# Two PSUM banks for the last down product, and an earlier place for the conditioning's tanh and SiLU

## Chip, cores and metric

The kernel runs on one core of a Trainium2 chip. The metric is the device time of one execution in microseconds. Seven runs of the kernel before had a median of 254.84 us, from 253.79 to 256.03 us. The profile shows one execution in detail; it took 254.04 us, and its span, the time from the first to the last profiled event, is 252.3 us.

## What is computed

One transformer block on 2048 tokens of width 448, in bf16, conditioned on one vector `c`:

```
mod = silu(c) @ w_mod                      # six vectors of 448: sa, ca, ga, sb, cb, gb
h = layernorm(x) * (1 + ca) + sa
x = x + ga * attention(h)                  # 16 heads of 28, four segments of 512 tokens,
                                           # causal softmax in a segment, linear memory between segments
h = layernorm(x) * (1 + cb) + sb
x = x + gb * ((sigmoid(h @ w_gate) * (h @ w_up)) @ w_down)     # 448 -> 1792 -> 448
```

Two places of it matter here. At the very start `silu(c)` has to be there before the first conditioning vectors can be made, and these are folded into the projection weights. At the very end the product with `w_down` gives the last rows of the output.

## The kernel before

**How the work is laid out.** The 2048 tokens are four segments of four tiles with 128 tokens each. TensorE, VectorE (DVE), ScalarE (ACT), GpSimd (POOL) and the DMA queues of SP (SyncE) and ACT are each given their instructions in the order in which the Python code runs; the order is written out by hand, and each engine works its own list strictly from the front. The ACT list holds both ScalarE's computations and the loads that ACT issues, so an ACT load that waits also holds back the ACT computations written behind it, and the other way round. In the middle of the kernel a list of filler jobs with costs (`fill`, `tick`, `later`) decides where projections and the gated product go between the attention steps; the change touches neither that list nor its costs.

**The start.** L106 and L104 issue the loads of `c` (tile `c_col`, on ACT) and of the first four tiles of `x` (tile `x_sb`: tiles 0 and 1 on SP, 2 and 3 on ACT). L120 loads the parts 1 and 0 of `w_mod` (tiles `wm1`, `wm0`), each half by SP and half by ACT. L151 to L153 load `A_wq` and `A_wk` into a corner of `wd_sb`: row blocks 0 and 1 of each by SP, blocks 2 and 3 of `A_wq` by ACT, and those of `A_wk` by SP. L139 and L140 load `A_wv`. L196 is `th = tanh(c/2)` on ScalarE. It is written behind all of these loads, so it stands behind ACT's two `A_wq` loads, and the table load that the first ScalarE function needs stands just ahead of it.

Meanwhile TensorE runs 20 matmuls on a constant (`warm_up`, L647) that no result depends on. DVE computes the LayerNorm statistics of the four tiles (L269 and L270, one pair for a tile), POOL turns them into 1/sqrt(var+eps) for two tiles at a time (L273 and L274), and DVE then runs `silu_ops` (L200 and L201: two operations on a 112x4 tile, which give `silu`). TensorE makes the first conditioning columns from `silu` and `wm1` (L228), DVE normalizes tiles 0 and 1 (L277), evacuates those columns (L240), normalizes tiles 2 and 3, and evacuates the second columns (L238, tile `sa_bf`). TensorE transposes the normalized tiles (L688), DVE scales the projection weights by the columns (`pad_copy`, L657) and copies transposed tiles (L306), TensorE multiplies `sa_bf` with the weights (`bias_rows`, L664), and the first projections follow (L343).

**DMA semaphores.** The loads share eight completion semaphores, taken in turn as the loads are written in the program. A load that takes a semaphore again waits until the earlier load with that semaphore has landed, and so do the engine and queue behind it. Which earlier load that is follows from the order in which the whole program is laid out, and is seen in the list of the built program's instructions.

**PSUM.** `ps_m` is a pool of four PSUM tiles of one bank each, which `m_f32` hands out in turn. A tile is handed out again when its readers have finished.

**The end.** `down(s, t)` multiplies the gated product of one tile of tokens with `w_down`: 14 matmuls (L574) into one PSUM tile `dp`, one DVE addition of the residual (L576), and one store (L577, on ACT in the last two segments). For the very last tile `n` is 2: columns 0 to 223 and then columns 224 to 447, each with 14 matmuls, an addition and a store of its own, both in the same `dp`.

Of the kernel before, what the change touches and what calls it, by code (L numbers as in the profile page):

```python
# [9 lines left out]
F32 = mybir.dt.float32  # L10
AF = mybir.ActivationFunctionType
# [6 lines left out]
def kernel(  # L18
# [16 lines left out]
    nc = tc.nc  # L35
# [7 lines left out]
    KP, NK = 112, 4  # L43
# [5 lines left out]
    scale = float(Dh) ** -0.5  # L49
# [10 lines left out]
    const = ctx.enter_context(tc.tile_pool(name="const", bufs=1))  # L60
# [6 lines left out]
    def m_f32(name):  # L67
        return ps_m.tile([P, 512], F32, tag="m", name=name)
# [23 lines left out]
    def need(*tags):  # L92
        for tag in tags:
            late_ = [d for d in deferred if d[3] == tag]
            if late_:
                print("forced", tag, len(late_), max(d[0] for d in late_) - clock[0])
            run_deferred(lambda d: d[3] == tag)


    c_col = const.tile([KP, NK], BF16)  # L100
# [14 lines left out]
    def load_wm(engs, j):  # L115
        t = wm_bufs[j % 2]
        n = NK // len(engs)
        for i, eng in enumerate(engs):
            k = slice(i * n, (i + 1) * n)
            eng.dma_start(t[:, 0:NK * D].rearrange("p (k n) -> p k n", n=D)[:, k, :], wmod_k[:, k, j * D:(j + 1) * D])  # L120
        return t

    wm_bufs = [wts.tile([KP, NK * D + DP - D], BF16, name=f"wm{i}") for i in range(2)]
    wm = {j: load_wm((nc.sync, nc.scalar), j) for j in (1, 0)}
    wq_sb = wts.tile([P, NK, H, HP], BF16)
    wk_sb = wts.tile([P, NK, H, HP], BF16)
    wv_sb = wts.tile([P, NK, D], BF16)
# [64 lines left out]
    coef = const.tile([P, 2, H], F32)  # L192


    th = const.tile([KP, NK], F32)
    nc.scalar.activation(th[:], c_col[:], AF.Tanh, scale=0.5)  # L196
    silu = const.tile([KP, NK], BF16)

    def silu_ops():
        nc.vector.tensor_scalar(th[:], th[:], 0.5, 0.5, op0=ALU.mult, op1=ALU.add)  # L200
        nc.vector.tensor_tensor(silu[:], th[:], c_col[:], ALU.mult)  # L201
# [13 lines left out]
    def mod_cols(jobs, cp=None):  # L215
        evac = cp is None
        cp = cp_of[0] = m_f32("cp") if evac else cp
        for j, vi in jobs:
            for kc in range(NK):
                for k in range(NK):  # L220
                    c0 = k * D + kc * P
                    if vi >= 2 and kc == NK - 1:
                        for r in (0, LW):
                            nc.tensor.matmul(cp[r:r + LW, vi * NK + kc:vi * NK + kc + 1], lhsT=wm[j][:, c0:c0 + LW],
                                             rhs=silu[:, k:k + 1], start=(k == 0), stop=(k == NK - 1),
                                             tile_position=(0, r))
                        continue
                    nc.tensor.matmul(cp[:, vi * NK + kc:vi * NK + kc + 1], lhsT=wm[j][:, c0:c0 + P],  # L228
                                     rhs=silu[:, k:k + 1], start=(k == 0), stop=(k == NK - 1))
        if evac:  # L230
            mod_evac(jobs)
# [331 lines left out]

    def down(s, t):
        need("wd")
        dp = m_f32("dps")
        i = s * TPS + t
        ot = work.tile([P, D], BF16, tag="ot", bufs=2)
        eng = nc.scalar if s >= NSEG - 2 else nc.sync
        n = 2 if i == NSEG * TPS - 1 else 1  # L570
        for h in range(n):
            c = slice(h * D // n, (h + 1) * D // n)
            for fc in range(NFC):
                nc.tensor.matmul(dp[:, c], lhsT=fT_of[(s, fc)][:, t * P:(t + 1) * P], rhs=wd_sb[:, fc, c],  # L574
                                 start=(fc == 0), stop=(fc == NFC - 1))
            nc.vector.tensor_tensor(ot[:, c], dp[:, c], x_sb[:, i, c], ALU.add)  # L576
            eng.dma_start(out_dram[i * P:(i + 1) * P, c], ot[:, c])  # L577
# [27 lines left out]
    def down_jobs(s):  # L605
        return [(NFC * MV, lambda t=t: down(s, t)) for t in range(TPS)]
# [66 lines left out]
    for t in range(TPS):  # L673
        ln0.stats(t)
        if t % 2:
            ln0.rstd(t - 1, t + 1)
    silu_ops()
    mod_cols(((1, 1),), warm[:, 2, :])
    for t in range(2):
        ln0.norm(t)  # L680
# [193 lines left out]
```

The softmax here doesn't subtract the row's maximum and nothing guards it: scores larger than these inputs give would overflow.

## Time and profile before

| what | value |
|---|---|
| median of seven runs | 254.84 us |
| the profiled execution | 254.04 us, span 252.3 us |
| TensorE matmuls busy | 240.4 us, 95% of the span |
| DVE, ACT, POOL busy | 173.6, 139.1, 73.9 us |
| granted TensorE clock | full in all 40 slices |
| DMA engines busy | 90% or more of each slice from 6.3 to 44 us, under half in nearly all after 57 us |
| `dps` matmuls of L574 | 238 recorded, 43.9 us |

Busy time says which engine the kernel leans on; it does not say what a change at one place is worth. For that one reads the timeline at that place: the start of each instruction, its length, and in square brackets how long the engine was idle just before it and what ended that. A row "x14" is fourteen instructions of one line merged. "ACTq" and "SPq" are the issue of DMAs, with the time that issuing takes; when the data lands is told by another view as a number of microseconds after the issue. Matmuls overlap in the pipeline, so a merged row's length is not the sum of its parts.

### The profile page before, as it was taken

The numbers are of one execution on the slowest core, as the hardware profiler recorded it, in microseconds if no ns is written. First come the engines' busy times: TensorE is split into PE (matmuls) and PEld (weight loads), VectorE is DVE, ScalarE is ACT, GpSimd is POOL, SyncE is SP. The second block draws the span as 40 slices with busy tenths as digits, with TensorE's granted clock in tenths as the row PEclk, the third lists the DMA queues.
The fourth block names the chain that finished last, engine by engine and source line by source line (L and its number), as shares of the span: only waits on it lengthen the run. The fifth ranks groups of instructions, "written<-read, shape, count | busy, mean of one in ns | idle before, by whom it ended". The sixth has DMA issues, their size and how long they took to land.

```text
span 252.3 us, 5315 instructions
## 1 busy us (share of the span) xinstructions
PE 240.4 (95%) x2059; PEld 114.5 (45%) x2083; DVE 173.6 (69%) x419; ACT 139.1 (55%) x173; POOL 73.9 (29%) x140
## 2 busy tenths in 40 slices
PE   7899998999987999999999999999999999999994
PEld 3434544446533435545443355454444455333453
DVE  6878799784887786589866766895555585544422
ACT  0458879978896977667285838543642300233200
POOL 4359144232553223344513141471120032000000
PEclk9999999999999999999999999999999999999999
DMA  5999999494034330103342110123110105000011
GB/s 149 284 256 245 355 279 128 87 190 66 3 62 68 62 43 2 23 0 63 80 97 42 26 23 0 25 42 88 50 22 3 21 3 137 19 0 0 3 36 36
DMA packets 41168, 19.66 MB, mean 78 GB/s; under 512 B 30008, under 2 KB 40248, under 8 KB 41144
## 3 DMA queue, kind: packets, MB, share of 16 engines
q1 hardware_dynamic: 38408, 17.61, 32.7%
q10 hardware_dynamic: 2736, 1.72, 2.3%
q8 instruction: 16, 0.26, 0.4%
q14 instruction: 8, 0.07, 0.1%
HBM read 10.67 MB, written 1.84 MB: 50 GB/s over the span
## 4 chain that ended last, share of the span: by engine, by line
PE 52%; DVE 7%; POOL 1%; issue 1%; DMA 1%; ACT 1%; DVEq 0%; POOLq 0%
PE ups L559 13%; PE dps L574 13%; PE gps L542 12%; PE gps L547 5%; PE acc L451 3%; PE pwo L510 2%; PE lg L424 2%; DVE fT L562 1%; DVE st L269 1%; DMA hT<-xn 1%; DVE x_sb L520 1%; DVE ot L576 1%; DVE t L482 1%; PE dM L397 1%; PE ups L547 1%
## 5 line engine op out<-in xcount | busy, mean ns | idle before, releaser
L427 ACT ACTIVATE pT<-lg 128x2048 bf16<-128x2048 f32 (+1 forms) x48 | 76.8, 1599 | 25.9 <-PE lg L424 25.5
L562 DVE SCALAR_TENSOR_TENSOR fT<-tt,ups 128x512 bf16<-128x512 f32 x56 | 37.3, 688 | 39.3 <-PE ups L559 37.5
L437 POOL TENSOR_SCALAR_AFFINE_SELECT pT<-pT 128x512 bf16<-128x512 bf16 x64 | 40.6, 650 | 69.1 <-ACT pT L427 69.1
L550 ACT ACTIVATE tt<-gps 128x512 f32<-128x512 f32 x56 | 30.4, 594 | 55.1 <-PE gps L547 55.1
L574 PE MATMUL dps<-wd_sb,fT 128*128 128x448 bf16 (+1 forms) x238 | 43.9, 341 | 0.5 <-DVE ot L576 0.5
L542 PE MATMUL gps<-hT,wg_sb 128*128 128x512 bf16 x155 | 40.1, 379 | 1.4 <-ACT vt L357 0.6
L559 PE MATMUL ups<-hT,wu_sb 128*128 128x512 bf16 x165 | 40.6, 381 | 0.4 <-issue 0.3
L574 PEld LDWEIGHTS <-fT 128*128 128x128 bf16 x238 | 22.9, 98 | 19.4 <-issue 0.6
L559 PEld LDWEIGHTS <-wu_sb 128*128 128x128 bf16 x168 | 14.1, 97 | 21.7 <-issue 7.9
L542 PEld LDWEIGHTS <-wg_sb 128*128 128x128 bf16 x168 | 15.6, 98 | 18.2 <-DVE hT L291 1.1
L451 PE MATMUL acc<-vt,pT 128*128 128x29 bf16 x640 | 18.6, 175 | 2.1 <-POOL pT L437 1.7
L269 DVE BATCH_NORM_STATS2 st<-x_sb 128x6 f32<-128x448 bf16 x32 | 19.7, 617 | 0.5
L451 PEld LDWEIGHTS <-pT 128*128 128x128 bf16 x640 | 17.6, 96 | 5.2 <-POOL pT L437 2.4
L547 PE MATMUL ups<-hT,wgu_sb 64*128 64x512 bf16 x56 | 17.8, 382 | 0.8 <-ACT tt L550 0.5
L273 POOL TENSOR_SCALAR rs<-mv 128x1 f32<-128x1 f32 (+2 forms) x21 | 5.2, 247 | 44.6 <-DVE mv L270 44.1
L424 PE MATMUL lg<-qT,kT 28*128 28x512 bf16 (+3 forms) x256 | 17.3, 302 | 0.2
L547 PE MATMUL gps<-hT,wgu_sb 64*128 64x512 bf16 x56 | 17.0, 381 | 0.1
L343 PE MATMUL pq<-hT,wq_sb 128*128 128x512 bf16 x59 | 16.3, 379 | 0.7 <-issue 0.3
L576 DVE TENSOR_TENSOR ot<-dps,x_sb 128x448 bf16<-128x448 f32 (+1 forms) x17 | 9.9, 592 | 9.6 <-PE dps L574 9.6
L343 PE MATMUL pq<-hT,wk_sb 128*128 128x512 bf16 x62 | 16.3, 379 | 0.1
L277 DVE TENSOR_SCALAR xn<-x_sb,mv,rs 128x448 bf16<-128x448 bf16 x32 | 14.4, 472 | 2.1 <-POOL rs L274 2.0
L274 POOL TENSOR_TENSOR rs<-rs,mhalf 128x1 f32<-128x1 f32 (+2 forms) x21 | 14.3, 682 | 1.7
(101 smaller groups left out, 256.2 us busy)
## 6 DMA issues: line engine op xcount, KB each, us to landing
wm<-in_w_mod_dram SPq DMA_DIRECT2D x4, 392.0 KB, 6.5
x_sb<-in_A_x_dram SPq DMA_DIRECT2D x3, 448.0 KB, 7.3
wd_sb<-in_B_w_down_dram SPq DMA_DIRECT2D x3, 448.0 KB, 9.0
wg_sb<-in_B_w_gate_dram SPq DMA_DIRECT2D x3, 448.0 KB, 10.3
wu_sb<-in_B_w_up_dram SPq DMA_DIRECT2D x3, 448.0 KB, 10.9
out_dram<-ot SPq DMA_DIRECT2D x8, 112.0 KB, 1.9
out_dram<-ot ACTq DMA_DIRECT2D x7, 112.0 KB, 1.7
wm<-in_w_mod_dram SPq DMA_DIRECT2D x2, 196.0 KB
```

The costliest lines, as they stand in the source:

```text
L269: nc.vector.bn_stats(st[:], self.srcs[i])
L343: nc.tensor.matmul(pq[:, 0:L], lhsT=head_cols(w_sb, k, hc), rhs=h[:, k, :], start=(k == 0), stop=(k == NK - 1))
L424: nc.tensor.matmul(lg[:, hs, wid:wid + nq], lhsT=kT[r, hc, kb * P:(kb + 1) * P], rhs=qT[r, hc, kb * P:L], start=True, stop=True, tile_posi ...
L427: nc.scalar.activation(pT[:, :, w0:w0 + wid], lg[:, :, 0:wid], AF.Exp, scale=scale)
L437: nc.gpsimd.affine_select(out=blk, in_=blk, compare_op=ALU.is_ge, fill=0.0, base=0, pattern=[[0, 4], [1, P]], channel_multiplier=-1)
L451: nc.tensor.matmul(accv[:, qb, hs, 0:ME], lhsT=pT[:, hs, c0:c0 + P], rhs=vt[:, kb, hc * 4 + hs, 0:ME], start=(kb == 0), stop=(kb == qb))
L542: nc.tensor.matmul(g[:, 0:L], lhsT=wg_sb[:, k, f], rhs=h[:, k, :], start=(k == 0), stop=False)
L547: nc.tensor.matmul(dst[:, 0:L], lhsT=wgu_sb[r:r + LW, f], rhs=h[r:r + LW, 3, :], start=first, stop=not first, tile_position=(r, 0))
L550: nc.scalar.activation(tt[:], g[:, 0:L], AF.Tanh, scale=0.5)
L559: nc.tensor.matmul(u[:, 0:L], lhsT=wu_sb[:, k, f], rhs=h[:, k, :], start=False, stop=(k == 2))
L562: nc.vector.scalar_tensor_tensor(ft[:], tt[:], 1.0, u[:, 0:L], op0=ALU.add, op1=ALU.mult)
L574: nc.tensor.matmul(dp[:, c], lhsT=fT_of[(s, fc)][:, t * P:(t + 1) * P], rhs=wd_sb[:, fc, c], start=(fc == 0), stop=(fc == NFC - 1))
```

## The change

Three edits. The tanh of the conditioning vector moves from behind all loads to just behind the `w_mod` loads, so that in ACT's list it stands ahead of the two `A_wq` loads. `silu_ops` moves in DVE's list from behind the statistics of tile 3 to behind those of tile 1 (and the POOL operations of tiles 0 and 1). And in `down` the PSUM tile is taken inside the loop over the halves, so that the last tile's two halves have a PSUM bank each. No instruction is added or removed.

```diff
     wm = {j: load_wm((nc.sync, nc.scalar), j) for j in (1, 0)}
+    th = const.tile([KP, NK], F32)
+    nc.scalar.activation(th[:], c_col[:], AF.Tanh, scale=0.5)
     wq_sb = wts.tile([P, NK, H, HP], BF16)
...
-    th = const.tile([KP, NK], F32)
-    nc.scalar.activation(th[:], c_col[:], AF.Tanh, scale=0.5)
     silu = const.tile([KP, NK], BF16)
...
     def down(s, t):
         need("wd")
-        dp = m_f32("dps")
         i = s * TPS + t
...
         for h in range(n):
             c = slice(h * D // n, (h + 1) * D // n)
+            dp = m_f32("dps")
             for fc in range(NFC):
                 nc.tensor.matmul(dp[:, c], lhsT=fT_of[(s, fc)][:, t * P:(t + 1) * P], rhs=wd_sb[:, fc, c],
                                  start=(fc == 0), stop=(fc == NFC - 1))
...
         ln0.stats(t)
         if t % 2:
             ln0.rstd(t - 1, t + 1)
-    silu_ops()
+        if t == 1:
+            silu_ops()
     mod_cols(((1, 1),), warm[:, 2, :])
```

## Prediction

> **What bounds the kernel now.** The page first. TensorE is busy for 95% of the span and the granted clock is full throughout, so what TensorE waits for at the two places of the change is nearly all that can be won or lost.
>
> ```profile
> PE 240.4 (95%) x2059; PEld 114.5 (45%) x2083; DVE 173.6 (69%) x419; ACT 139.1 (55%) x173; POOL 73.9 (29%) x140
> PEclk9999999999999999999999999999999999999999
> L574 PE MATMUL dps<-wd_sb,fT 128*128 128x448 bf16 (+1 forms) x238 | 43.9, 341 | 0.5 <-DVE ot L576 0.5
> ```
>
> The last row says that all the down matmuls together have 0.5 us of idle time before them, and one releaser: the DVE addition of L576. The timeline of the end (start, length, then the idle time before and what ended it) shows where that is.
>
> ```profile
> 247.24 0.39 DVE L576 TENSOR_TENSOR ot<-dps,x_sb 128x224 bf16<-128x224 f32 x1 [0.72 <-PE dps L574]
> 247.68 1.50 PE L574 MATMUL dps<-wd_sb,fT 128*128 128x224 bf16 x14 [0.48 <-DVE ot L576]
> 249.22 0.39 DVE L576 TENSOR_TENSOR ot<-dps,x_sb 128x224 bf16<-128x224 f32 x1 [1.59 <-PE dps L574]
> ```
>
> TensorE finishes the first half, stands still while DVE adds it, and only then begins the second half. The chain of waits runs through exactly these three rows to the end.
>
> At the start I read the timeline of the first 16 us, engine by engine.
>
> ```profile
> 4.80 0.36 ACTq L152 DMA_DIRECT2D wd_sb<-in_A_wq_dram  x1
> 6.18 0.53 ACTq L153 DMA_DIRECT2D wd_sb<-in_A_wq_dram  x1
> 6.42 0.35 SPq L152 DMA_DIRECT2D wd_sb<-in_A_wk_dram  x1
> 6.74 1.28 ACT L196 ACT_TABLE_LOAD   x1 [6.74 <-DMA x_sb<-in_A_x_dram]
> 8.04 0.20 ACT L196 ACTIVATE th<-c_col 112x4 f32<-112x4 bf16 x1
> 8.05 0.18 DVE L270 BATCH_NORM_AGGREGATE mv<-st 128x2 f32<-128x6 f32 x1
> 8.27 0.17 DVE L200 TENSOR_SCALAR th<-th 112x4 f32<-112x4 f32 x1
> 8.56 0.70 DVE L277 TENSOR_SCALAR xn<-x_sb,mv,rs 128x448 bf16<-128x448 bf16 x2
> 8.64 0.88 POOL L274 TENSOR_TENSOR rs<-rs,mhalf 128x2 f32<-128x2 f32 x1
> 8.69 0.54 PE L228 MATMUL warm<-silu,wm 112*128 112x1 bf16 x16 [0.99 <-DVE silu L201]
> 9.56 0.70 DVE L277 TENSOR_SCALAR xn<-x_sb,mv,rs 128x448 bf16<-128x448 bf16 x2
> 10.72 0.16 DVE L238 CAST sa_bf<-warm 128x4 bf16<-128x4 f32 x1 [0.46 <-PE warm L228]
> 12.32 0.32 DVE L657 TENSOR_SCALAR wq_sb<-wd_sb,cols 64x448 bf16<-64x448 bf16 x1
> ```
>
> The tanh is late because ACT first has to issue two loads, which themselves wait. TensorE's 0.99 us of idle time looks like the prize, but DVE is the engine without slack here: it works almost without a gap from 5.26 us to 10.26 us, and what it gains counts. From L238 on, DVE runs nearly back to back to 14.3 us and TensorE follows it.
>
> **The end: one PSUM bank for each half.** Removed: the wait of 0.48 us. The second half's first matmul then follows the first half's last at the matmul pitch. Its PSUM tile is the one that `down` of the last segment's first tile used, and the addition that frees it ran at 240.6 us (an L576 row of the same timeline, 0.62 us long), 6 us earlier. So the 14 matmuls begin near 247.22 instead of 247.68: 0.46 us. The first half's addition (0.39 us) now lies beside the 1.50 us of matmuls; without that cover it would cost what it does now. The additions do not collide on DVE (the first ends at 247.63, the second would begin near 248.76), nor do the stores on ACT's queue: an L577 issue takes 0.34 us, the first at about 247.7 and the second at 249.1. What is late next is unchanged: the second addition, its store, 1.6 us to landing, the end. The bounds are 0.40 and 0.48; an addition of 0.62 us runs beside the matmuls of the next tile in the whole tiles just before, where L574 shows no gap. Taken: -0.46.
>
> **The start: ACT.** The tanh waits for `c_col`, which landed 4.0 us after its issue at 0.79. In the list of the built program the table load carries no wait, so it runs when the second `w_mod` issue is over (1.80 + 1.00 = 2.80) and ends at 4.1; the tanh then runs from 4.8 to 5.0, where it was done at 8.24. [...] The trace has 1.28 us and the tanh 0.02 us behind it. [...]
>
> **The two ACT loads behind the tanh.** More changes here than their place. The semaphores are taken in another order, so the loads wait for other landings. Block 2 of `A_wq` waited for `c_col` (issued 4.80); it now waits for SP's half of `wm1`, which released SP's L152 at 6.42: 1.6 us later. Block 3 waited for `x` tiles 2 and 3 (6.18); it now waits for SP's half of `wm0`, which landed between 6.4 and 8.2 (SP's L139, which waited for it, was issued at 8.21 straight behind the issue before it): 0.2 to 2.0 us later. In return the three `A_wk` loads wait for `c_col` and the two `x` loads and go to about 4.8, 5.2 and 6.2 from 4.98, 6.42 and 7.60, and `A_wv` to 7.6 from 8.21. They all lie ahead of their users by more than before. Block 2 is read at 11.74 and block 3 at 12.32 (L657), and by TensorE's L664 from 11.68 on. Before, these two took 4.9 and 4.6 us from issue to landing. With those rows block 2 lands at 11.3, in time, and block 3 at 11.0 to 12.8, up to 0.5 us late. [...] The last earlier one on ACT, its half of `wm0`, had landed by 8.8 (SP's L140, which waited for it, was issued at 8.83). [...] Taken: 0; the far end +0.5 stays for the range.
>
> **DVE, POOL and TensorE at the start.** In the statistics the next operation starts 0.10 us after an aggregate starts. Before, the first SiLU operation started 0.22 us after one (8.05 to 8.27), since the tanh ended at 8.24. Now: aggregate of tile 1 at 6.59, SiLU at 6.69 and 6.90 (they stood 0.21 apart), statistics of tile 2 at 6.98 instead of 6.69, +0.29. The aggregate of tile 3 starts at 8.34 and the norm of tile 0 at 8.44 instead of 8.56: -0.12. POOL's power for tiles 2 and 3 is moved by +0.29 and ends at 9.81 instead of 9.52, so the second pair of norms goes from 9.56 to 9.85 and ends at 10.55. This would be a loss, but DVE had idled 0.46 us behind that pair, up to 10.72, waiting for TensorE's second L228. On TensorE the first L228 can run at 7.7, behind the warm-up, instead of 8.69. This alone wins nothing, as DVE's evacuation of it (9.27) stands behind the norms of tiles 0 and 1. But the transposes of tile 0 then no longer queue behind it: they start at 8.9, when the norm is done (8.44 + 0.39), instead of 9.09. The second L228 lies 1.04 us after (10.13 - 9.09), at 9.94, and ends at 10.48. L238 runs when both are done: 10.55 instead of 10.72. Taken: -0.15. All that follows hangs on L238; the next tiles of `x` landed at 14.97 (9.37 + 5.6) and are read at 15.52, so they don't hold this up. Bounds: -0.3 (the 0.12, and the idle 0.46 less the 0.29) and +0.2 (POOL's late power with no gain on TensorE).
>
> **The sum.** -0.46 - 0.15 = -0.61. The profiled execution took 254.04 us (span 252.3, 1.7 us around it), and would take 253.4. It is 0.8 us under the median, so against the median the forecast is 254.84 - 0.61 = 254.2 us, -0.24%. A difference of 0.5% (1.27 us) is about what a measurement of this kernel can tell from no change.
>
> **The rivals.** (1) The `A_wq` loads are too late: slower. If block 3 took as long as SP's first `A_wq` load did (issued 2.37, 6.8 us), it would land at 15.0 and hold L657 by 2.7 us: 254.84 + 2.7 - 0.46 = 257.1 us. It decides from a landing at 12.8 on, where it eats the gain of the end, and shows as slower from 14.0. For it: the DMA engines are full from 4 to 16 us. Against: the output stores' 1.6 us, and that all other weights come earlier. 0.10. (2) The start gives nothing: POOL's 0.29 us reaches L238, or a later wait takes up the 0.15. Then 254.84 - 0.46 + 0.1 = 254.5 us. 0.25. (3) The halves still run one behind the other, because the second one's wait is for something other than the bank. Against: the profile names the addition, and TensorE reads nothing that it writes. 254.84 - 0.15 = 254.7 us. 0.05. (4) More is won: the start gives up to the 0.99 us that TensorE idled, 254.84 - 0.46 - 0.99 = 253.4 us or a little below. For it: the `A_wk` and `A_wv` loads come earlier. Against: DVE's chain. 0.12. My forecast has 0.48.
>
> **How the numbers follow.** The seven runs lie 2.2 us apart, so a median is uncertain by some 0.4 us, about as much as the effect. Faster by over 0.5% needs rival 4, or the forecast with luck: 0.15. Slower by over 0.5% is most of rival 1, and a little scatter: 0.09. The rest, 0.76, is within. The range goes from rival 4's 253.4, less 0.1, to 255.4, which takes in rival 1 up to a delay of 1 us and rivals 2 and 3 with scatter.
>
> **What would show it.** In the profile after: the second half of `dps` with no idle time behind an addition; the tanh near 4.8; SiLU near 6.7; the norms of tiles 2 and 3 near 9.85; L238 near 10.55; the 64-row L657 near 12.2 with no wait. An L657 or L664 that waits for a DMA is rival 1. If L238 is not before 10.72, the start gave nothing. If the time is under 253.3 or over 255.4, a wait elsewhere has changed that I haven't seen.

## The result, and the profile after

| | before | after |
|---|---|---|
| median | 254.91 us (64 executions) | 254.19 us (27 executions) |
| ratio, 95% interval | | 0.9967 [0.9951, 0.9982] |
| the profiled execution | 254.04 us, span 252.3 us | 253.69 us, span 251.9 us |

The change takes 0.72 us, 0.3%, off the median. That is a real difference, since the interval does not hold 1, though it is smaller than the 0.5% that the prediction took for about what a measurement of this kernel can tell. In this and the later tables, four executions that were over 1.5% longer than the fastest of their kernel (one of the kernel before beside e5 to e8, one of e9, two of e10) count in the medians and not in the ratios.

The page of the changed kernel first (its busy times are within 0.7 us of before on every engine): the granted clock by slice, and the row of the down matmuls.

```profile
PEclk9999999999997999999999999999999999999999
...
L574 PE MATMUL dps<-wd_sb,fT 128*128 128x448 bf16 (+1 forms) x238 | 43.7, 341 | 0.0
```

The last row has no idle time in front of it any more: the edit at the end did what it says. The clock row has a 7 in the thirteenth slice, which the kernel before did not have in its profiled execution. That is a cost from elsewhere, and it comes up again below.

The end, in the timeline (start, length, and in brackets the idle time before and what ended it). The first row is the last whole tile's addition in the kernel before, the others are of the changed kernel:

```profile
245.90 0.62 DVE L576 TENSOR_TENSOR ot<-dps,x_sb 128x448 bf16<-128x448 f32 x1 [2.02 <-PE dps L574]
...
246.17 0.62 DVE L576 TENSOR_TENSOR ot<-dps,x_sb 128x448 bf16<-128x448 f32 x1 [2.02 <-PE dps L574]
247.51 0.39 DVE L576 TENSOR_TENSOR ot<-dps,x_sb 128x224 bf16<-128x224 f32 x1 [0.72 <-PE dps L574]
248.85 0.39 DVE L576 TENSOR_TENSOR ot<-dps,x_sb 128x224 bf16<-128x224 f32 x1 [0.95 <-PE dps L574]
```

The three additions of the changed kernel are evenly spaced: 1.34 us, and 1.34 us. Before, the first step was 1.34 us too (245.90 to 247.24) and the second 1.98 us (247.24 to 249.22). From the last whole tile's addition to the last half's it was 3.32 us and is 2.68 us. The gain is **0.64 us**, more than the 0.48 us of idle time that the profile showed. The other 0.16 us is the tail of a matmul. Without a stop the 14 matmuls of a half take 1.34 us, so one begins every 96 ns. A single one is longer than that: 259 ns in the mean (in e10's row further down), so several overlap. Behind the stop the fourteen stand alone and take 13 times 96 ns and once 259 ns, together 1.50 us, the length of their row in the kernel before. This working uses ends of matmuls, which the profile models; the 1.98 us and 1.34 us between DVE's additions don't depend on it.

The start, engine by engine, in the timeline of the changed kernel. Its line numbers are two above those of before between L126 and L196 and one above from L677 on; L155 is the `A_wq` load of block 3. The last row is the first projection in the kernel before.

```profile
4.66 0.20 ACT L126 ACTIVATE th<-c_col 112x4 f32<-112x4 bf16 x1 [0.54 <-DMA c_col<-in_c_dram]
...
6.70 0.14 DVE L200 TENSOR_SCALAR th<-th 112x4 f32<-112x4 f32 x1
...
8.02 0.53 ACTq L155 DMA_DIRECT2D wd_sb<-in_A_wq_dram  x1
...
8.97 0.72 POOL L274 TENSOR_TENSOR rs<-rs,mhalf 128x2 f32<-128x2 f32 x1
...
9.72 0.70 DVE L277 TENSOR_SCALAR xn<-x_sb,mv,rs 128x448 bf16<-128x448 bf16 x2 [0.55 <-POOL rs L274]
...
10.46 0.16 DVE L238 CAST sa_bf<-warm 128x4 bf16<-128x4 f32 x1
...
12.48 0.33 DVE L657 TENSOR_SCALAR wq_sb<-wd_sb,cols 64x448 bf16<-64x448 bf16 x1 [0.33 <-DMA wd_sb<-in_A_wq_dram]
...
13.01 1.16 PE L343 MATMUL pq<-hT,wq_sb 128*128 128x512 bf16 x4
...
12.85 1.16 PE L343 MATMUL pq<-hT,wq_sb 128*128 128x512 bf16 x4
```

Read it as a hand-over. The tanh, SiLU and the norms stand where the step-by-step working put them, and L238 comes at 10.46 where it was at 10.72: 0.26 us won. But two lines further down L657 has a bracket that it did not have before: it waits 0.33 us for block 3 of `A_wq`, which ACT issued at 8.02 instead of 6.18. L657 then starts at 12.48 (before 12.32) and the first projection at 13.01 (before 12.85). The 0.26 us won at L238 have become a loss of 0.16 us.

A third place lies far from both edits. In the kernel before, TensorE is idle for 0.20 us near 43 us, ahead of the projections of segment 2. These need transposes that SP issues behind the last of the weight loads. The first two rows are of the kernel before, the other two of the changed one: the issue of the last weight load, and the projections that need the transposes.

```profile
30.17 0.47 SPq L740 DMA_DIRECT2D wgu_sb<-in_B_w_up_dram  x1
...
42.94 1.02 PE L343 MATMUL pq<-hT,wq_sb 128*128 128x512 bf16 x3 [0.20 <-PE lg L424]
```

```profile
29.20 0.47 SPq L741 DMA_DIRECT2D wgu_sb<-in_B_w_up_dram  x1
...
42.83 1.04 PE L343 MATMUL pq<-hT,wq_sb 128*128 128x512 bf16 x3
```

The last weight load goes out 0.97 us earlier, the transposes land after 2.5 us instead of 3.8 us (median), and the wait of 0.20 us is gone. The bracket of before names TensorE's own L424; that the wait was for the transposes I take from their landing, and e1's row below names them. An ACT instruction at 51 us, which stood 0.16 us behind its time of before when compared at 19 us, stands 0.09 us ahead of it: 0.25 us won here.

The fourth place is the clock. The first row is TensorE's in the timeline of the changed kernel. The windows below it give, for each microsecond, its length, then busy time and count of PE, PEld, DVE, ACT and POOL, then the granted clock, the DMA share and GB/s.

```profile
76.56 1.20 PE L451 MATMUL acc<-vt,pT 128*128 128x29 bf16 x40 [1.69 <-POOL pT L437]
...
76.00:77.00 1.00, 0.44 (x18) 0.47 (x19) 0.91 (x3) 1.00 (x1) 0.53 (x1) 1.00 0.38 78
77.00:78.00 1.00, 1.00 (x31) 0.78 (x28) 0.19 (x1) 1.00 (x2) 0.32 (x1) 0.51 0.27 55
78.00:79.00 1.00, 1.00 (x4) 0.23 (x2) 0.60 (x2) 0.13 (x1) 0.91 (x2) 0.50 0.65 129
79.00:80.00 1.00, 1.00 (x4) 0.34 (x4) 1.00 (x5) 0.53 (x1) 0.00 (x0) 0.50 1.18 144
80.00:81.00 1.00, 0.95 (x4) 0.33 (x3) 0.93 (x5) 0.00 (x0) 0.00 (x0) 0.78 0.62 5
```

For some 3.4 us the clock is at half. Just before, TensorE had stood idle for 1.69 us and then run forty matmuls of 29 columns. The same instruction compared at 51 us and at 97 us moves from 0.09 us ahead to 0.28 us behind: 0.37 us lost in this execution.

The profiled pair therefore adds up to +0.16 (start) - 0.25 (near 43 us) + 0.37 (clock) - 0.64 (end) = -0.36 us, and the spans went from 252.3 to 251.9 us.

The clock was not brought by the change. Every execution's mean granted clock is recorded: 0.998 to 1.000 in those that I count as full, 0.993 or less in the others, as in the profiles with such a stretch. The table has the median (and the number of executions) of each kind. The kernel before was run again beside each set of experiments; of its 154 executions there, 34 were at full clock, of the changed kernel's 50 (its first runs are 28 in this count, one more than in the median above) 17 were.

| executions | full clock | the others |
|---|---|---|
| changed kernel, first runs | 253.53 us (9) | 254.52 us (19) |
| changed kernel again (e4) | 253.38 us (8) | 254.38 us (14) |
| kernel before, beside e1 to e4 | 254.20 us (15) | 254.86 us (52) |
| kernel before, beside e5 to e8 | 253.99 us (10) | 254.82 us (29) |
| kernel before, beside e9 and e10 | 254.85 us (8) | 254.99 us (13) |
| kernel before, beside e11 and e12 | 255.09 us (1) | 255.45 us (26) |

Like with like and beside each other (e4 and the kernel before in the third row), the changed kernel is faster by 0.82 us at full clock and by 0.48 us otherwise. The lost clock goes with 0.66 to 1.00 us in four of the six rows, but with 0.14 us in one, so it is not the same everywhere. The profiled execution of before, with a full clock, was one of the better ones, and the pair of profiles shows less than the medians do.

### The profile page after: what moved, and what is told of

Read it like the earlier page. It is cut to its first block, busy times and chain, and to the rows that moved or that the text cites. A ratio compares the mean times of both kernels' runs of the same rounds, so it can differ in the third digit from the quotient of the medians.

```text
span 251.9 us, 5315 instructions
## 1 busy us (share of the span) xinstructions
PE 241.1 (96%) x2059; PEld 115.0 (46%) x2083; DVE 173.8 (69%) x419; ACT 139.0 (55%) x173; POOL 73.8 (29%) x140
## 4 chain that ended last, share of the span: by engine, by line
PE 52%; DVE 7%; POOL 1%; issue 1%; DMA 1%; ACT 1%; DVEq 0%; POOLq 0%
PE ups L559 13%; PE dps L574 13%; PE gps L542 12%; PE gps L547 5%; PE acc L451 3%; PE pwo L510 2%; PE lg L424 2%; DVE fT L562 1%; DVE st L269 1%; DMA hT<-xn 1%; DVE x_sb L520 1%; DVE t L482 1%; PE dM L397 1%; PE ups L547 1%; PE mem L475 1%
## 5 line engine op out<-in xcount | busy, mean ns | idle before, releaser
L424 PE MATMUL lg<-qT,kT 28*128 28x512 bf16 (+3 forms) x256 | 17.3, 302 | 0.4 <-ACT pT L427 0.2
```

Of the source, the lines that this page charges most:

```text
L424: nc.tensor.matmul(lg[:, hs, wid:wid + nq], lhsT=kT[r, hc, kb * P:(kb + 1) * P], rhs=qT[r, hc, kb * P:L], start=True, stop=True, tile_posi ...
```

## The experiments

My theory after the result was: the end gives 0.64 us every time; the start gives less than nothing at block 3; and the rest of the difference is the moved wait near 43 us and the clock. The rivals were that the start gives the gain, that the end's 0.64 us is partly something else, and that splitting the last tile is not worth its cost once the banks are apart. Ratios are to the kernel before on the same chip, with 95% intervals.

### Each half of the change alone, one load on another queue, and the change again

```diff
 e1_end_only: the kernel before, with
-        dp = m_f32("dps")
         for h in range(n):
             c = slice(h * D // n, (h + 1) * D // n)
+            dp = m_f32("dps")
 e2_start_only: the changed kernel, without that edit
 e3_block3_on_SP: the changed kernel, with
-    other.dma_start(st[0:LW,3,:]...)
+    nc.sync.dma_start(st[0:LW,3,:]...)
 e4_after_again: the changed kernel
```

> The two PSUM banks at the end alone; the start as in the kernel before. Theory A (the gain of the end is the whole 0.48 us that TensorE stood still for the addition): L574 shows no idle time behind L576, the last addition starts 0.46 us earlier than before against the same earlier instruction (the one ahead of it still takes 0.39 us), the start is as before (L238 at 10.7, L657 of block 3 at 12.3), and the time is 0.46 us below the kernel before, ratio 0.998. Rival B (the end is no bank wait, something else holds the second half): idle time of about 0.5 us stays ahead of the second half, ratio 1.000.

> The two edits of the start alone; both halves of the last tile in one PSUM bank as before. Theory A (the start wins 0.26 us up to L238 and loses 0.4 us again to block 3 of A_wq; later the earlier weight loads give 0.25 us back near 43 us): L238 near 10.46, L657 of block 3 near 12.48 behind a wait of 0.3 us for its DMA, the first projection near 13.0 (before 12.85), the first L343 after 42 us about 0.1 us earlier than before, and 0.48 us of idle time in L574. Time -0.1 us against before, ratio between 0.998 and 1.001. Rival B (the wait for block 3 in the one profile after was chance): no wait ahead of L657, first projection near 12.6, ratio 0.998 or less.

> The changed kernel, but block 3 of A_wq is issued by SP straight behind blocks 0 and 1, where it waits for c_col (landed near 4.8) and not for a half of wm0. Theory A (block 3 came late because its issue waited for another load's landing, to 8.02, and then took over 4 us beside SP's queue): it is there by 11 us, L657 of block 3 starts near 12.07 with no wait, the first projection near 12.6 instead of 13.0, and the time is 0.4 us below the changed kernel, 1.0 below the kernel before, ratio to before near 0.996. Rival B (the DMA engines are full from 4 to 16 us, so another block takes its place): L657 or L664 waits as long for block 2 of A_wq or a block of A_wk, the first projection stays near 13.0, ratio as the changed kernel's.

> The changed kernel once more, on the same chip as its parts, with a profile of its own. Theory A: the wait of 0.3 us ahead of L657 for block 3, the first projection near 13.0, no idle time in L574; the half clock from 77 to 81 us that the first profile had is chance and need not come back, and without it the last addition starts near 248.5 instead of 248.85. Rival B (the half clock comes from the change): it comes back at the same place. Time about 0.6 us below before, ratio 0.9975.

| kernel | median us (executions) | ratio | span of the profiled one |
|---|---|---|---|
| e1, end only | 254.71 (14) | 0.9996 [0.9972, 1.0021] | 252.1 |
| e2, start only | 254.51 (22) | 0.9993 [0.9979, 1.0007] | 253.1 |
| e3, block 3 on SP | 253.79 (22) | 0.9971 [0.9957, 0.9985] | 252.5 |
| e4, the change again | 254.06 (22) | 0.9963 [0.9944, 0.9981] | 252.4 |

The time of either half by itself can't be told from no change: the intervals are as wide as the effects. (The two ratios together would make 0.9989, and the change has 0.9967; their intervals allow it.) The rows can be told apart. In e1's timeline the last addition:

```profile
248.97 0.39 DVE L576 TENSOR_TENSOR ot<-dps,x_sb 128x224 bf16<-128x224 f32 x1 [0.95 <-PE dps L574]
```

It comes 2.68 us behind the last whole tile's, just as in the changed kernel; e3 has 2.69 and e4 2.68 us, and e2, without the edit, 3.32 us and the old 0.48 us in front of the second half:

```profile
248.48 1.50 PE L574 MATMUL dps<-wd_sb,fT 128*128 128x224 bf16 x14 [0.48 <-DVE ot L576]
```

The end is worth 0.64 us whatever goes on before it. In e1 the wait near 43 us was 0.61 us instead of 0.20 us, which moved everything behind it by 0.39 us: the span fell by only 0.2 us.

```profile
43.31 1.02 PE L343 MATMUL pq<-hT,wq_sb 128*128 128x512 bf16 x3 [0.61 <-DMA hT<-xn]
```

In e2's and e3's timelines the row of block 3:

```profile
12.80 0.33 DVE L657 TENSOR_SCALAR wq_sb<-wd_sb,cols 64x448 bf16<-64x448 bf16 x1 [0.65 <-DMA wd_sb<-in_A_wq_dram]
```

```profile
12.07 0.32 DVE L657 TENSOR_SCALAR wq_sb<-wd_sb,cols 64x448 bf16<-64x448 bf16 x1
12.60 1.17 PE L343 MATMUL pq<-hT,wq_sb 128*128 128x512 bf16 x4
```

With the start alone (e2), ACT issued block 3 at 8.38 us and L657 waited 0.65 us. All profiles with the changed start and block 3 on ACT have the wait: 0.33, 0.65, 0.17 (e4), and in the experiments below 0.30 and 0.19 us. With the same load on SP it went out at 4.66 us, the wait is gone and the first projection starts at 12.60 us, 0.25 us earlier than before and 0.41 us earlier than after. So the start's gain of 0.26 us is real, and block 3 takes it back. It was not a slow queue that made block 3 late: on SP's queue it took 5.3 us from issue to landing, on ACT's 4.3 to 4.5 us to L657 in the five profiles. The issue 3.4 us earlier brought it in time.

```profile
wd_sb<-in_A_wq_dram SPq DMA_DIRECT2D x1, 56.0 KB, 5.3
```

In the medians of all executions e3 does not show it clearly (0.27 us below e4's, ratio 0.9971 against 0.9963, and the intervals overlap). But e3 was at full clock in 3 of its 22 executions and e4 in 8. Sorted by clock, e3 has 252.93 against e4's 253.38 us at full clock and 253.87 against 254.38 us otherwise, 0.45 and 0.51 us less, near the 0.41 us of the rows. The profiled execution of e3 does not show the gain at its end:

```profile
30.62 0.47 SPq L741 DMA_DIRECT2D wgu_sb<-in_B_w_up_dram  x1
...
43.80 1.02 PE L343 MATMUL pq<-hT,wq_sb 128*128 128x512 bf16 x3 [1.32 <-DMA hT<-xn]
```

In this execution the last weight load went out at 30.62 us, the transposes behind it needed 4.9 us instead of 2.5 us, and TensorE waited 1.32 us. What was won at 13 us was lost at 43 us, and more, in this execution.

### The three causes taken away, and the last tile in one piece

```diff
 e5_up_loads_late: e3, with the w_up pieces taken out of early_loads, and
-    fill.extend(j2[:8])
+    fill.extend(spread(j2[:8], late_loads, 2))
 e6_no_idle_at_75: the changed kernel, with ahead of a pv product
+            if u == (1, 1):
+                for _ in range(7):
+                    nc.tensor.matmul(acc[:, 0:D], lhsT=ident[:], rhs=wv_sb[:, 0, :], start=True, stop=True)
 e7_all_three: e3, e5 and e6 together
 e8_last_tile_whole: the changed kernel, with
-        n = 2 if i == NSEG * TPS - 1 else 1
+        n = 1
```

> The kernel with block 3 on SP, and the four w_up loads moved in SP's list from ahead of segment 2's hT transposes to behind them (into the projections of segment 2, near 50 us; first use 81 us). Theory A (near 43 us TensorE waits for the hT transposes, which queue in SP's ring behind the last weight loads; this wait was 1.3 us in the profile with block 3 on SP, 0.3 before, none in the changed kernel): the transposes land in 2.5 us, no wait of L343 for DMA near 43 us, and the 0.25 us won at 15 us are still there at 50 us. Time 0.3 to 1.0 us below the kernel with block 3 on SP (253.8), ratio to before near 0.994. Rival B (the late transposes are an effect of the DMA engines as such, and the loads moved hold up the transposes of 50 to 75 us instead): the wait turns up at another L343, L355 or L542, time as with block 3 on SP or above.

> The changed kernel with seven matmuls on constants written ahead of the attention product of segment 1, second head group, into the PSUM tile that this product then overwrites: they fill most of TensorE's 1.7 us of idle time near 75 us (a wait for POOL's masks) and add no result. Theory A (the half clock from 77 to 81 us, seen in the profiles of the changed kernel and in the mean clock of about 0.99 of three runs in four of the kernel before, follows from that idle time, and costs 0.5 to 0.7 us): the granted clock stays full there, mean clock 1.00 in nearly all runs, median 253.5, 0.6 below the changed kernel, ratio to before near 0.9945. Rival B (the half clock has nothing to do with the idle time): the share of runs with a mean clock of 0.99 stays near two in three, and the time is the changed kernel's or up to 0.3 us longer.

> The changed kernel with block 3 on SP, the w_up loads behind the transposes and the seven filling matmuls. If each theory holds the gains add: 0.4 us at the start, up to 0.3 near 43 us, 0.5 near 77 us, so 1.0 to 1.2 us below the changed kernel: 253.0 us, ratio to before near 0.993. If the rivals hold it is the changed kernel's time, 254.1.

> The changed kernel with the last tile in one piece: 14 matmuls of 448 columns, one addition, one store. Theory A (what the separate bank won is the gap that the split itself had made; the split costs TensorE about 0.3 us, as 28 matmuls of 224 columns take about 2.9 us and 14 of 448 take 2.65, and saves 0.23 us of the last addition and 0.1 of the last store): no gap, the last addition takes 0.62 us, and the span ends within 0.1 us of the changed kernel's, seen from the same earlier instruction. Rival B (the split with two banks is worth what it was made for): the end is 0.3 us or more later than the changed kernel's.

| kernel | median us (executions) | ratio | span |
|---|---|---|---|
| e5, `w_up` later | 257.48 (7) | 1.0093 [1.0058, 1.0127] | 255.8 |
| e6, seven matmuls more | 253.48 (6) | 0.9945 [0.9925, 0.9964] | 251.8 |
| e7, all three | 256.49 (17) | 1.0069 [1.0049, 1.0089] | 254.7 |
| e8, last tile whole | 254.31 (22) | 0.9986 [0.9972, 1.0000] | 251.7 |

**e5** was a miss. The wait near 43 us went, with the transposes there landing after 2.4 us, so it was those loads that had made them late. But the loads that went later now stand in front of the transposes that `dM` needs. The waits of e5 between 45 and 75 us (total, times, longest):

```profile
PE dM L397 <- DMA pk<-e: 1.9, 1, 1.9
```

Putting a load elsewhere in the same queue only chose another victim, and a costlier one: e5's median is 3.7 us above e3's (on another chip). Behind that idle time of 1.9 us its clock was also at half from 63.4 to 66.9 us, besides the stretch near 82 us. In the profiles ACT's instructions of e5 stand 1.4 us ahead of the same ones of e3 at 50 us, 0.8 us behind at 62 us, 2.3 us behind at 70 us and 3.2 us behind at 140 us; the second stretch of half clock explains only a part of the last 0.9 us. e7 carries the same wait (1.6 us) and the same first stretch; its second one is gone.

**e6** puts seven matmuls of 448 columns in front of the forty narrow ones, into the PSUM tile that these then start over. Its timeline and its clock:

```profile
76.53 1.50 PE L449 MATMUL acc<-wv_sb,ident 128*128 128x448 bf16 x7 [1.59 <-DVE t L485]
77.86 1.16 PE L454 MATMUL acc<-vt,pT 128*128 128x29 bf16 x40
```

```profile
PEclk9999999999999999999999999999999999999999
```

The seven did not fill the idle time: they waited for their PSUM tile, and 1.59 us of idle time stayed. Yet the clock was full, in the profile and in all six executions, where the kernel before had it in 10 of the 39 beside them. They move the forty from 76.56 to 77.86 us, but little of that reaches the end: 253.48 us stands beside the 253.38 us of e4's executions at full clock (on another chip). So the idle time alone does not bring half clock here. I take it that what counts is how little the array does in that stretch, idle time and narrow matmuls together; that the forty come later is the other thing that the seven change, and no run tells the two apart. In the changed kernel the clock fell at 77.0 us, 2.1 us after TensorE's last matmul of 384 columns had ended at 74.9 us (2.6 us in e4), and it stood at 0.50 for about 3.4 us. How little work brings it down, and over what time, no run shows.

**e8** asks what splitting is worth now. Its last two additions:

```profile
245.64 0.62 DVE L576 TENSOR_TENSOR ot<-dps,x_sb 128x448 bf16<-128x448 f32 x1 [2.02 <-PE dps L574]
248.29 0.62 DVE L576 TENSOR_TENSOR ot<-dps,x_sb 128x448 bf16<-128x448 f32 x1 [2.02 <-PE dps L574]
```

In one piece it takes 2.65 us to the start of the last addition, in halves with two banks 2.68 us. Half-width matmuls cost TensorE 0.03 us for the tile, not the 0.3 us that I had thought. The split then gains 0.23 us at the addition, 0.39 against 0.62 us, and a little at the store, which landed after 1.5 against 1.7 us. With its place at the last whole tile's addition set equal to that of before (-0.26 us in e8, +0.27 us after), the span would be 252.0 us for e8 and 251.6 us for the changed kernel. Split in two banks is better by 0.3 to 0.4 us; split in one bank, as before, it was worse than not split at all, by the same reckoning 252.3 against 252.0 us.

### The wait for the bank, in every tile

```diff
 e9_all_split_one_bank: the kernel before, with    e10_all_split_two_banks: e1, with
-        n = 2 if i == NSEG * TPS - 1 else 1
+        n = 2
```

> The kernel before with every tile's down product in two halves, all in one PSUM bank per tile: the suspected wait sixteen times instead of once, with fifteen more additions and stores. Theory A (each second half waits 0.48 us for the addition of the first, since both are in one bank): idle time of about 7 us in L574 behind L576 (16 times 0.45), and a time about 7 us above that of the same kernel with two banks. Where other work stands between the halves it would be less; none does in the list. Rival B (only the last tile has the wait): the two kernels differ by 0.5 us.

> As the one with every tile in two halves in one bank, but each half with a PSUM bank of its own. Theory A: no idle time in L574 behind L576; against the kernel before it is longer by what the split costs (about 0.3 us of matmuls for each of 15 tiles, 4 to 5 us) less the 0.48 us of the last tile, ratio near 1.015; against the one-bank form about 7 us shorter. Rival C (a second bank for each tile takes the PSUM tiles from the gated product, which then waits): idle time moves to L542 or L547, and the two forms come out alike.

| kernel | median us (executions) | ratio | span |
|---|---|---|---|
| e9, one bank | 281.01 (4) | 1.0978 [1.0899, 1.1057] | 281.0 |
| e10, two banks | 256.91 (18) | 1.0060 [1.0039, 1.0081] | 253.4 |

The waits of e9, the page of e10, and two rows of e9's timeline:

```profile
PE dps L574 <- DVE ot L576: 20.5, 16, 3.9
```

```profile
L574 PE MATMUL dps<-wd_sb,fT 128*128 128x224 bf16 x448 | 44.5, 259 | 0.3 <-DVE t L463 0.2
```

```profile
121.77 2.77 PE L574 MATMUL dps<-wd_sb,fT 128*128 128x224 bf16 x14 [3.83 <-DVE ot L576]
...
128.58 1.50 PE L574 MATMUL dps<-wd_sb,fT 128*128 128x224 bf16 x14 [0.48 <-DVE ot L576]
```

This is the mechanism at large, with nothing else changed between the two kernels. The profiled execution of e9 was the longest of its four (282.99 us, the shortest took 277.84 us), so I read the waits from it, not the time. In one bank, all sixteen tiles make TensorE wait for the addition, 20.5 us together; in two banks 0.3 us is left. Where DVE is free, the price is the same 0.48 us as at the end. In the middle the addition stands behind other work in DVE's list, and TensorE, which works its list in order, stands with it for up to 3.9 us. I had expected 7 us of waits for e9, which counted sixteen times the price at the free place; that was too little by a factor of three. Its span is 27.6 us above e10's; the 7 us that the waits leave over I put down to the tails of the matmuls and to half clock (0.72 in the mean from 120 to 132 us), without having separated them. For e10 I had expected 4 to 5 us more than e1; it was 2.0 us over the kernel before on its chip.

### What the experiments point to, and the kernel before with the seven matmuls

```diff
 e11_block3_and_fill: e3 and the seven matmuls of e6
 e12_before_and_fill: the kernel before and the seven matmuls of e6
```

> The changed kernel with block 3 of A_wq on SP and with the seven filling matmuls of segment 1's second head group (they add no result). Theory A (the seven matmuls keep the clock full by the work they are, behind the idle time of 1.6 us, which they don't fill; the runs of the kernel with block 3 on SP that had the full clock took 252.9 us): mean clock 1.00 or 0.998 in nearly all runs, median 253.0, ratio to before 0.993, if the wait for the transposes near 43 us is short in most runs. Rival B (that wait of 1.3 us is the rule with block 3 on SP, and eats what the start wins): L343 waits about 1 us for DMA near 43 us and the median is that of the changed kernel with the filling matmuls, 253.5, or above.

> The kernel before with only the seven filling matmuls (they add no result). Theory A (the half clock near 77 us is a matter of how little the array does between 75 and 78 us, and the kernel before had it in three runs of four): mean clock 1.00 in nearly all runs, median 254.2, ratio 0.9975. Rival B (the effect on the changed kernel was chance, six runs): the share of runs with a mean clock of 0.99 stays at three in four, and the median at 254.8.

| kernel | median us (executions) | ratio | span |
|---|---|---|---|
| e11 | 253.22 (6) | 0.9915 [0.9883, 0.9947] | 251.3 |
| e12 | 254.40 (22) | 0.9976 [0.9954, 0.9999] | 252.4 |

e11 is 0.85% faster than the kernel before, and its interval lies below the changed kernel's [0.9951, 0.9982]. It was at full clock in all six executions, e12 in 20 of 22 (254.19 us) and the kernel before beside them in 1 of 27. With the clock the same in both, the change and block 3 on SP are worth 254.19 - 253.22 = 0.97 us. The rows give nearly that: at 19 us e11 stands 0.41 us ahead of e12 (-0.26 and +0.15 us against before), and the end gives its 0.64 us; together 1.05 us. In front of the last addition DVE is idle for 0.95 us in e11 (first row) and for 1.59 us in e12: the 0.64 us once more.

```profile
248.22 0.39 DVE L579 TENSOR_TENSOR ot<-dps,x_sb 128x224 bf16<-128x224 f32 x1 [0.95 <-PE dps L577]
...
249.31 0.39 DVE L579 TENSOR_TENSOR ot<-dps,x_sb 128x224 bf16<-128x224 f32 x1 [1.59 <-PE dps L577]
```

## Why the prediction was right, point by point

The forecast was 254.2 us and the median is 254.19 us. The mechanism of the end carried it. That the two agree so closely is luck: the difference was forecast as -0.61 and measured as -0.72 us, the end gave more than its term, the start lost where its term won, and two effects were not in the sum.

- **The end: right mechanism, too small.** The term was -0.46 and measured -0.64 us. The mis-sized step is "begin near 247.22 instead of 247.68". The sentence before it has the second half follow "at the matmul pitch", which counts from the start of the matmul ahead, but 247.22 is counted from its end at 247.20. From its start it would be 247.20 - 0.26 + 0.10 = 247.04, and 0.64 us. Eight profiles with the edit have 2.68 or 2.69 us where three without it (before, e2, e12) have 3.32 or 3.33. That the addition hides beside the matmuls, that additions and stores don't collide, and that the last addition and store come next, held.
- **The start up to L238: right.** Tanh forecast at 4.8, measured 4.66; SiLU 6.69 and 6.70; norm of tile 0 8.44 and 8.43; second pair of norms 9.85 and 9.72; L238 10.55 and 10.46. The difference in the last two is POOL: its power was moved by 0.33 us (worked out: 0.29) but took 0.72 us instead of 0.88. The table load was the trace's 1.28 us and waited for nothing. The tanh came 0.55 us after its end, and the profile names the landing of `c_col` for 0.54 us of that.
- **Block 3: the step that failed.** The rows of before gave a landing at 11.0 to 12.8, "up to 0.5 us late", and the term is "Taken: 0". No run shows that 0: in all five profiles with the changed start and block 3 on ACT, L657 waits for it, for 0.17 to 0.65 us. It was issued at 8.02 us, where the working had 8.2, and held L657 until 12.48 us: 4.5 us, where the row of before had 4.6 and would have put it at 12.6. This is also the sign that the prediction named for its rival 1. Against that rival it held the output stores' 1.6 us, which are the wrong neighbours: they find the DMA engines nearly free (a mean share of 0.13 from 246 to 252 us, in both profiles), and this load shares them with SP's loads, which keep them full there (from 8.02 to 12.5 us in the changed kernel they are busy 90% or more in 39 of 40 slices; the packets of SP's queue took 96% of the engines' time, those of ACT's 15%). The working counted only the loads ahead of it on ACT's own queue and put SP's at nothing. How much of the 4.5 us is due to SP's loads no run separates. Cost: instead of -0.15 the first projection moved by +0.16 us.
- **Rival 1 came true at a small size.** Its point of decision was a landing at 12.8; e2 reached it (L657 at 12.80 us), the changed kernel didn't. Rival 2, a start that gives nothing, is what happened at 13 us, by way of a "later wait". Rivals 3 and 4 did not come: the halves no longer wait, and the 0.99 us were not to be had.
- **Not foreseen: the transposes near 43 us.** With the changed start and block 3 on ACT, the last weight load was issued between 28.67 and 29.37 us in five profiles, and none of them waits there. e3 and e11, with block 3 on SP, had 30.62 us and a wait, and 29.44 us and none. With the old start it was between 29.57 and 30.17 us, and two of five profiles wait. So the changed start tends to bring the weights out earlier, and was worth 0.25 us in the pair shown; this is seen, not forced by an experiment (e5 forces only the other half, that the loads make the transposes late), and e3 shows that it can be lost again. Why the loads' times differ from one execution to the next is open.
- **Not foreseen: the clock.** The page of before showed it full in all slices, and I took that for the kernel's nature. It is so in 22% of its executions, and the profile had caught one of them.

## What to carry to other kernels

Moving a computation past a DMA issue moves the issue as well (here block 3's from 6.18 to 8.02 us), and may change which landing it waits for: take its time to land from the row of that load in that stretch (4.6 us here), not from a load that finds the queues empty (1.6 us). A stop of TensorE for a reader costs the idle time and then some (0.64 us for 0.48 us here), and where the reader stands behind other work on its engine, several times that (up to 3.83 us in e9); a second PSUM bank took it away here (0.48 us to none at the end, 20.5 us in e9 to 0.3 us in e10). Where tenths of a microsecond matter, sort the executions by granted clock first: here that alone was up to 1.0 us, more than the whole change, and it hid the gain of e3.

## What was unexpected of the hardware

- The clock went to half for about 3.4 us although TensorE was idle for only 1.4 to 1.9 us before (1.69 us in the changed kernel, 1.4 and 1.9 us in e5); at 77 us forty matmuls of 29 columns behind that did not hold it up, and with seven of 448 columns ahead of them it stayed full in 32 of 34 executions (e6, e11, e12). The mean clock was 0.993 or less in 120 of 154 executions of the kernel before and in 33 of 50 of the changed one.
- A load of 56 KB took 4.6 us from issue to landing on ACT's queue (before) and 5.3 us on SP's (e3) where the DMA engines were busy 90% or more of each slice, and a store of the same size 1.5 to 1.6 us where their mean share was 0.13. The transposes near 43 us took 2.5 us in the changed kernel, and 3.8 to 4.9 us in the three profiles in which TensorE waited for them.
- Halving the columns of 14 matmuls from 448 to 224, with twice as many of them, cost TensorE 0.03 us for the tile.
